# Attention decode and a gated feed-forward on one core: the last transfers are cut anew, the first query weights ride in K's row, and x's columns are made on chip

## The chip, the core and the metric

One core of one Trainium2 chip. The metric is the device time of one execution in microseconds (us). All data are float32. TensorE (PE) multiplies matrices into PSUM, VectorE (DVE) reduces and multiplies, ScalarE (ACT) does exp, square root and copies, GpSimd (POOL) sets constants, and SyncE (SP) issues nearly all transfers from HBM into SBUF.

## The reference

One token x (640 numbers) goes through an attention block over a cache of 8192 positions with 32 heads of 192, and then through a gated feed-forward of width 1536:

```
h   = x + (softmax(q K^T / sqrt(192)) V) @ wo        q = layernorm(x) @ wq, per head
h2  = h + (relu(g) * u) @ W_down                     g = layernorm(h) @ W_gate
                                                     u = layernorm(h) @ W_up
```

The caches K and V are 32 x 8192 x 192 each, so nearly all bytes are K and V, read once. The weights wq and wo are 640 x 6144 and 6144 x 640, W_gate and W_up 640 x 1536, W_down 1536 x 640.

## The kernel before

The host packs the inputs into rows, one for each of the 128 partitions. For a head there is a K row (array kk, 12288 columns, 6144 KB over all partitions) and a V row (array vv, 14208 columns, 7104 KB): V as 12 blocks of 1024 columns, then 960 columns of output weights, then 960 columns of query weights for the *next* head. The last head's V row (v0) has no query weights. A small array w0 holds the first head's query weights and x as 5 columns, and ww holds the feed-forward's weights in the order up, gate, down.

In SBUF one long tile, big, holds a K row (kt) and two V rows (vts[0], vts[1]) in turn. Head n works like this:

- TensorE makes the query from the weights at the end of the V row before (query, 5 matmuls), VectorE picks its columns out (columns), ScalarE masks them into qs (masks).
- When the K row has landed, TensorE computes the scores: 24 matmuls, each of which is two instructions in the profile, into the PSUM tile sp. The semaphore sp counts it.
- TensorE then does the output of the head *before* (output): a small matmul into po, VectorE's combine, and 8 matmuls with the output weights into acc, which counts the semaphore wo.
- VectorE takes the maximum, ScalarE the exp, and VectorE multiplies p with the 12 V blocks, one instruction each (ttr, the costly line of VectorE). The query columns of the next head come between blocks 5 and 6.

The order of the transfers is written out in sync_fn. SP issues K row n+1 when sp has counted n (the K tile is free) and V row n+1 when wo has counted n. All these transfers go into one queue and are moved in that order. Before the loop stand w0, the first K row and the first V row; after it comes the end:

- the last K row in two halves (semaphores k and k2), for which the scores wait half by half;
- the last V row in two pieces: its first JV = 7 blocks, then the other 5 with the output weights (semaphores vb and vb1);
- ww in six pieces at CUTS, issued when the scores and the output of the head before are done, since they overwrite kt and vts[0].

At the end, after the last block, the block's closing barrier passes, the last output goes into acc, ScalarE copies it to h4, the layer norm's mean and TensorE's products follow: project for up (20 matmuls into one half of sp), project for gate (20 more into the other half), VectorE's gu and its transpose guT, and 48 matmuls for down. weights() makes TensorE wait for the piece of ww that a column range begins. idle() issues matmuls whose result nobody uses. ScalarE copies the result to o4, and SP and ScalarE store it.

At the start VectorE builds constants, waits for w0 (semaphore vb) and computes the layer norm of x from the 5 columns xT with TensorE's help; x also comes as 4 rows of 160 (xrow, by ScalarE's queue) to start the sum in acc.

Of the kernel before, what the change touches and what calls it, by code (L numbers as in the profile page):

```python
# [57 lines left out]

def mha_decode_reglu_kernel(nc, x, w0, kk, vv, v0, ww, out):
    names = ("xr", "k", "k2", "va", "vb", "vb1", "qd", "qs", "sp", "mp", "pt", "m1", "rs",  # L60
             "pl", "q", "op", "po", "o", "o2", "wo", "cst", "st", "ffn0", "ffn1", "ffn2", "ffn3", "ffn4",
             "ffn5", "h4", "hm", "hc", "hr", "pu", "us", "pg", "gu", "pd", "pool", "dve")
    stored, s_o4 = (nc.alloc_semaphore("e_" + n) for n in ("out", "o4"))
# [4 lines left out]
    def sb(name, shape):  # L68
        return nc.alloc_sbuf_tensor(name, shape, F32).ap()
# [20 lines left out]
    st = sb("st", [P, 16])  # L90
# [31 lines left out]

    xT = vt2[:, 2 * VW:2 * VW + DJ]

    def ttr(eng, dst, a, b, scale, res):
# [3 lines left out]
    def sync_fn(sy):  # L129
        def load_k(h, n, dst=kt, c=slice(0, KW), sem="k"):  # L130
            if n is not None:
                sy.wait_ge(s["sp"], n)
            sy.dma_start(dst[:, c], kk[h][:, c]).then_inc(s[sem], 16)  # L133
# [6 lines left out]
        sy.dma_start(vt2[:, VW + KW + WO:2 * VW + DJ], w0).then_inc(s["vb"], 16)  # L140
        load_k(0, None)
        load_v(0, None, 0)
        sy.sem_inc(s["k2"], 16 * (H - 1))
        sy.sem_inc(s["vb1"], 16 * (H // 2))
        with sy.Fori(1, H - 2, 2) as i:
            load_k(i, i)
            load_v(i, i, 1)
            load_k(i + 1, i + 1)
            load_v(i + 1, i + 1, 0)
        load_k(H - 1, H - 1, c=slice(0, KW // 2))  # L150
        load_k(H - 1, None, c=slice(KW // 2, KW), sem="k2")
        sy.wait_ge(s["wo"], H - 1)
        for c0, c1, n in ((0, JV * SG, "vb"), (JV * SG, KW + WO, "vb1")):
            sy.dma_start(vts[1][:, c0:c1], v0[:, c0:c1]).then_inc(s[n], 16)
        sy.wait_ge(s["wo"], H)
        sy.wait_ge(s["sp"], H)
        for i, (c0, c1) in enumerate(zip(CUTS, CUTS[1:])):
            sy.dma_start(big[:, c0:c1], ww[:, c0:c1]).then_inc(s[f"ffn{i}"], 16)  # L158

# [60 lines left out]
    def vector_fn(v):  # L220
# [122 lines left out]
    def mm(dst, lhsT, rhs, start, stop, **kw):  # L343
        return nc.tensor.matmul(dst, lhsT, rhs, start=start, stop=stop, **kw)  # L344

    def weights(c0, n):
        if c0 in CUTS:
            nc.tensor.wait_ge(s[f"ffn{CUTS.index(c0)}"], 16)
        return big[:, c0:c0 + n]

    def project(c0, w0, done):
        for j in range(DJ):
            if w0 + j * F == CUTS[2]:
                idle(QB // 2)
            for g in range(NQ):
                ins = mm(sp[g * Q:(g + 1) * Q, c0:c0 + FG], hc[:, j, :], weights(w0 + j * F + g * FG, FG),
                         j == 0, j == DJ - 1)
# [19 lines left out]
    def tensor_fn(t):  # L377
# [6 lines left out]
        def scores():  # L384
            for u in range(NU):
                if u:
                    yield
# [6 lines left out]
            yield  # L394
# [17 lines left out]
        def k_wait(i, b, name):  # L412
            t.wait_ge(s[name], i * 16 + 16 * b if b else i * 16)
# [15 lines left out]
    def idle(n):  # L429
        mm(pt[:, 0:n], ident, p[:, 0:n], True, True)  # L430

    def tensor_end(t):
# [31 lines left out]

def _pack(x, k, v, wq, wo, up, gate, down):

# [3 lines left out]
    vv = _np.empty((H - 1, P, VW), v.dtype)  # L470
    v0 = _np.empty((P, KW + WO), v.dtype)
    w0 = _np.empty((P, WQ + DJ), v.dtype)
    w = wq.reshape(P, DJ, H, DH)
    o = wo.reshape(H, DH, D)
    w0[:, 0:WQ] = w[:, :, 0, :].reshape(P, WQ)
    w0[:, WQ:] = x.reshape(P, DJ)
    for h in range(H):
# [8 lines left out]
        if h < H - 1:  # L486
            r[:, KW + WO:] = w[:, :, h + 1, :].reshape(P, WQ)
    ww = _np.concatenate([a.reshape(P, -1) for a in (up, gate, down)], axis=1)
    return w0, kk, vv, v0, ww

# [22 lines left out]
```

## Time and profile before

| | |
|---|---|
| median of 3 runs | 1038.33 us (1038.3 to 1038.48) |
| the profiled execution, its own time | 1038.14 us |
| its span, first to last instruction | 1036.9 us |
| busy | PE 438.0 us (42%), DVE 525.2 us (51%), ACT 74.5 us (7%), POOL 2.8 us |
| moved | 445.98 MB, mean 430 GB/s |
| chain that ended last | DMA 76%, PE 23% |

The profile's times count from the span's start. A "busy" share is an average over the whole span. "us to landing" of a transfer counts from its issue by SP until its last bytes have landed, and so includes the time that it stands in the queue behind others. PEclk is the clock that TensorE was granted, as a part of full speed. A matrix instruction with float32 data appears twice in the profile, so 24 matmuls are 48 instructions.

### The profile page before, as it was taken

The numbers are of one execution on the slowest core, as the hardware profiler recorded it, in microseconds if no ns is written. First come the engines' busy times: TensorE is split into PE (matmuls) and PEld (weight loads), VectorE is DVE, ScalarE is ACT, GpSimd is POOL, SyncE is SP. The second block draws the span as 40 slices with busy tenths as digits, with TensorE's granted clock in tenths as the row PEclk, the third lists the DMA queues.
The fourth block names the chain that finished last, engine by engine and source line by source line (L and its number), as shares of the span: only waits on it lengthen the run. The fifth ranks groups of instructions, "written<-read, shape, count | busy, mean of one in ns | idle before, by whom it ended". The sixth has DMA issues, their size and how long they took to land.

```text
span 1036.9 us, 7438 instructions
## 1 busy us (share of the span) xinstructions
PE 438.0 (42%) x2746; PEld 201.2 (19%) x2746; DVE 525.2 (51%) x1162; ACT 74.5 (7%) x174; POOL 2.8 (0%) x18
## 2 busy tenths in 40 slices
PE   4255343344443344443443443443433553433536
PEld 2122121122121121111221111221211221211203
DVE  1644465644555544556544556444656444656472
ACT  1000000000000000000000000000000000000001
POOL 1000000000000000000000000000000000000000
PEclk8566666666655666655666655666656666656667
DMA  9999999999999999999999999999999999999998
GB/s 402 450 423 432 432 427 449 420 428 432 434 449 420 449 430 432 432 420 451 419 432 432 431 449 420 427 434 436 446 420 451 423 432 432 424 451 420 427 435 346
DMA packets 10532, 445.98 MB, mean 430 GB/s; under 512 B 1176, under 2 KB 1184, under 8 KB 1568
## 3 DMA queue, kind: packets, MB, share of 16 engines
q1 hardware_dynamic: 10516, 445.92, 99.6%
q8 instruction: 3, 0.05, 0.0%
q14 instruction: 1, 0.01, 0.0%
q10 hardware_dynamic: 12, 0.00, 0.0%
HBM read 445.91 MB, written 0.00 MB: 430 GB/s over the span
## 4 chain that ended last, share of the span: by engine, by line
DMA 76%; PE 23%; issue 0%; SPq 0%; DVE 0%; ACT 0%
DMA big<-in_kk_dram 72%; PE sp L344 23%; DMA big<-in_ww_dram 3%; SPq L133 0%; SPq L158 0%; PE pq L344 0%; PE acc L344 0%; SPq L140 0%; DVE junk L126 0%; PE po L344 0%; ACT o L340 0%; DVE o L126 0%
## 5 line engine op out<-in xcount | busy, mean ns | idle before, releaser
L126 DVE CUSTOM_DVE_ANT_0 big<-big,p 128x1024 f32<-128x1024 f32 x384 | 444.9, 1220 | 146.5 <-DMA big<-in_vv_dram 145.3
L344 PE MATMUL sp<-big,qs 128*32 128x512 f32 x1536 | 239.9, 789 | 342.9 <-DMA big<-in_kk_dram 338.4
L344 PE MATMUL pq<-big,xn 128*128 128x192 f32 x320 | 113.4, 540 | 154.2 <-DMA big<-in_vv_dram 152.3
L344 PEld LDWEIGHTS sp<-big,qs 128*32 128x32 f32 x1536 | 55.9, 140 | 513.4 <-DMA big<-in_kk_dram 359.7
L126 DVE CUSTOM_DVE_ANT_0 junk<-blk,po,rl 128x8 f32<-128x8 f32 x66 | 11.9, 218 | 265.5 <-PE po L344 265.5
L344 PEld LDWEIGHTS pq<-big,xn 128*128 128x128 f32 x320 | 97.9, 331 | 157.0 <-DMA big<-in_vv_dram 155.0
L303 ACT ACTIVATE o<-side,o 128x64 f32<-128x64 f32 x33 | 11.5, 348 | 479.2 <-DVE o L126 479.2
L315 ACT ACTIVATE qs<-pick,q 128x64 f32<-128x64 f32 x33 | 11.5, 348 | 410.3 <-DVE q L126 410.3
L321 ACT ACTIVATE p<-sp,m 128x1024 f32<-128x1024 f32 x32 | 35.6, 1113 | 47.9 <-DVE m L259 47.9
L257 DVE TENSOR_REDUCE mp<-sp 128x1 f32<-128x1024 f32 x32 | 39.0, 1220 | 0.0
L344 PE MATMUL pl<-rs,share 128*128 128x1 f32 x64 | 16.5, 327 | 51.9 <-ACT p L321 51.9
L261 DVE RECIPROCAL rl<-pl 128x1 f32<-128x1 f32 x32 | 5.4, 169 | 59.0 <-PE pl L344 59.0
L344 PE MATMUL acc<-big,o 128*32 128x160 f32 x528 | 28.8, 316 | 15.3 <-DVE o L126 15.3
L126 DVE DVE_READ_ACCUMULATOR2_ANT op<- 128x1 f32 x384 | 31.4, 82 | 0.0
L344 PEld LDWEIGHTS pl<-rs,share 128*128 128x128 f32 x64 | 13.8, 268 | 58.0 <-ACT p L321 58.0
L344 PE MATMUL po<-op,same 128*128 128x12 f32 x66 | 13.1, 272 | 16.0 <-PEq L452 16.0
L344 PEld LDWEIGHTS po<-op,same 128*128 128x128 f32 x66 | 10.0, 191 | 42.9 <-issue 26.8
L259 DVE TENSOR_REDUCE m<-pt 128x1 f32<-128x128 f32 x32 | 9.3, 292 | 13.3 <-PE pt L408 13.3
L344 PEld LDWEIGHTS acc<-big,o 128*32 128x32 f32 x528 | 10.6, 108 | 25.8 <-DVE o L126 18.4
L408 PE MATMUL pt<-ident,mp 128*128 128x128 f32 x32 | 10.3, 323 | 8.9 <-DVE mp L257 8.9
L126 DVE CUSTOM_DVE_ANT_0 junk<-ident,pq 128x128 f32<-128x128 f32 x33 | 9.3, 282 | 3.7 <-PE pq L344 3.7
L316 ACT ACTIVATE qs<-pick,q 128x32 f32<-128x32 f32 x33 | 10.1, 307 | 0.0
(78 smaller groups left out, 73.8 us busy)
## 6 DMA issues: line engine op xcount, KB each, us to landing
big<-in_vv_dram SPq DMA_DIRECT2D x31, 7104.0 KB, 38.8
big<-in_kk_dram SPq DMA_DIRECT2D x31, 6144.0 KB, 23.6
big<-in_kk_dram SPq DMA_DIRECT2D x2, 3072.0 KB, 19.5
big<-in_ww_dram SPq DMA_DIRECT2D x1, 3840.0 KB, 20.3
big<-in_v_dram SPq DMA_DIRECT2D x1, 3584.0 KB, 30.2
big<-in_v_dram SPq DMA_DIRECT2D x1, 3040.0 KB, 37.1
big<-in_ww_dram SPq DMA_DIRECT2D x1, 2304.0 KB, 25.5
big<-in_ww_dram SPq DMA_DIRECT2D x1, 2176.0 KB, 30.2
```

Source lines behind the costliest of these rows:

```text
L126: return eng.tensor_tensor_reduce(out=res, in0=a, in1=b, scale=scale, scalar=0.0, op0=ALU.mult, op1=ALU.add, accum_out=dst)
L257: v.reduce_max(mp, sp, axis=AX.X).then_inc(s["mp"])
L259: v.reduce_max(m1, pt[:, 0:P], axis=AX.X, negate=True).then_inc(s["m1"])
L261: v.reciprocal(rl, pl[:, 0:1])
L303: a.mul(o2, side, o[:, 1:2]).then_inc(s["o2"])
L315: a.mul(qs[:, 0:2, :], pk[:, 0:2, :], q[:, 0:1])
L316: a.mul(qs[:, 2, :], pk[:, 2, :], q[:, 1:2]).then_inc(s["qs"])
L321: a.activation(p, sp, AF.Exp, bias=m1, accum_out=rs).then_inc(s["rs"])
L344: return nc.tensor.matmul(dst, lhsT, rhs, start=start, stop=stop, **kw)
L408: t.transpose(pt[:, 0:P], mp.to_broadcast([P, P]), ident).then_inc(s["pt"])
```

## The change

*The long tile is laid out anew*: vts[1], then kt, then vts[0]. The query weights at the end of vts[1] and kt are now neighbours, and so are vts[1]'s output weights and the space behind them.

*The start.* w0 is gone. The first K row comes with the first head's query weights ahead of it, as one transfer k0 (13248 columns, 6624 KB) on the semaphore vb. x's columns are made on chip: VectorE multiplies the mask quad with xrow into a new tile xd, and five one-column matmuls with ones put x's columns into po, from which the layer norm reads.

*The end.* The last K row is one transfer. The last V row is cut at JV = 10 blocks, and its second piece now carries the up weights behind the output weights (10688 columns). That piece reaches into kt, so SP waits for the last scores (sp at H) before it, and no longer before ww. ww holds gate and down alone, in four pieces. project takes the up weights without a wait, and the filler ahead of gate's fourth row of matmuls is gone.

SP's queue at the start and at the end, before (names are tile <- input array, then partitions x columns; the first V row and the loop's transfers lie between the two pieces):

```order
L140 DMA big<-in_w_dram 128x965
L133 DMA big<-in_kk_dram 128x12288
...
L133 DMA big<-in_kk_dram 128x6144 [waits e_sp]
L133 DMA big<-in_kk_dram 128x6144
L154 DMA big<-in_v_dram 128x7168 [waits e_wo]
L154 DMA big<-in_v_dram 128x6080
L158 DMA big<-in_ww_dram 128x7680 [waits e_sp,e_wo]
L158 DMA big<-in_ww_dram 128x4608
L158 DMA big<-in_ww_dram 128x4352
L158 DMA big<-in_ww_dram 128x3840
L158 DMA big<-in_ww_dram 128x1920
L158 DMA big<-in_ww_dram 128x640
```

and of the change:

```order
L141 DMA big<-in_k_dram 128x13248
...
L134 DMA big<-in_kk_dram 128x12288 [waits e_sp]
L152 DMA big<-in_v_dram 128x10240 [waits e_wo]
L154 DMA big<-in_v_dram 128x10688 [waits e_sp]
L157 DMA big<-in_ww_dram 128x8960 [waits e_wo]
L157 DMA big<-in_ww_dram 128x3840
L157 DMA big<-in_ww_dram 128x1920
L157 DMA big<-in_ww_dram 128x640
```

The wait for the scores has moved from ww to the second V piece, and 7680 columns of up weights have moved ahead of ww's first wait.

TensorE's order at the feed-forward, before, from the last output's mean to the first down matmuls:

```order
L344 MATMUL pt<-hs,ones 128x1 [waits e_h4]
L344 MATMUL sp<-big,hc 32x384 [waits e_ffn0,e_hc]
L344 MATMUL sp<-big,hc 32x384 x3
L344 MATMUL pl<-st,ones 128x1 [waits e_st]
L344 MATMUL sp<-big,hc 32x384 x16
L344 MATMUL sp<-big,hc 32x384 [waits e_ffn1]
L344 MATMUL sp<-big,hc 32x384 x11
L344 MATMUL pt<-p,ident 128x256
L344 MATMUL sp<-big,hc 32x384 [waits e_ffn2]
L344 MATMUL sp<-big,hc 32x384 x7
```

and of the change:

```order
L347 MATMUL pt<-hs,ones 128x1 [waits e_h4]
L347 MATMUL sp<-big,hc 32x384 [waits e_hc]
L347 MATMUL sp<-big,hc 32x384 x3
L347 MATMUL pl<-st,ones 128x1 [waits e_st]
L347 MATMUL sp<-big,hc 32x384 x16
L347 MATMUL sp<-big,hc 32x384 [waits e_ffn0]
L347 MATMUL sp<-big,hc 32x384 x19
```

Up no longer waits for a piece of ww, gate waits for one piece instead of two, and the filler within gate is gone.

The diff, cut to its core:

```diff
-JV = 7
-GATE, DOWN, FW = DJ * F, 2 * DJ * F, 2 * DJ * F + FJ * D
-CUTS = (0, GATE, GATE + 3 * F, DOWN + 2 * D, DOWN + 8 * D, DOWN + 11 * D, FW)
+JV = 10
+UP = DJ * F
+VL = KW + WO + UP
+GATE, DOWN, FW = 0, DJ * F, DJ * F + FJ * D
+CUTS = (0, DOWN + 2 * D, DOWN + 8 * D, DOWN + 11 * D, FW)
...
-    big = sb("big", [P, KW + 2 * VW + DJ])
-    kt, vt2 = big[:, 0:KW], big[:, KW:]
-    vts = [vt2[:, i * VW:(i + 1) * VW] for i in range(2)]
+    big = sb("big", [P, VW + KW + VW])
+    kt = big[:, VW:VW + KW]
+    vts = [big[:, VW + KW:], big[:, 0:VW]]
+    upw, ffn = big[:, KW + WO:VL], big[:, VL:VL + FW]
     xrow = sb("xrow", [NQ, DG])
+    xd = sb("xd", [NQ, DJ, NQ, Q])
...
-        sy.dma_start(vt2[:, VW + KW + WO:2 * VW + DJ], w0).then_inc(s["vb"], 16)
-        load_k(0, None)
+        sy.dma_start(big[:, KW + WO:VW + KW], k0).then_inc(s["vb"], 16)
         load_v(0, None, 0)
...
-        load_k(H - 1, H - 1, c=slice(0, KW // 2))
-        load_k(H - 1, None, c=slice(KW // 2, KW), sem="k2")
+        load_k(H - 1, H - 1)
         sy.wait_ge(s["wo"], H - 1)
-        for c0, c1, n in ((0, JV * SG, "vb"), (JV * SG, KW + WO, "vb1")):
-            sy.dma_start(vts[1][:, c0:c1], v0[:, c0:c1]).then_inc(s[n], 16)
+        sy.dma_start(big[:, 0:JV * SG], v0[:, 0:JV * SG]).then_inc(s["vb"], 16)
+        sy.wait_ge(s["sp"], H)
+        sy.dma_start(big[:, JV * SG:VL], v0[:, JV * SG:VL]).then_inc(s["vb1"], 16)
         sy.wait_ge(s["wo"], H)
-        sy.wait_ge(s["sp"], H)
         for i, (c0, c1) in enumerate(zip(CUTS, CUTS[1:])):
-            sy.dma_start(big[:, c0:c1], ww[:, c0:c1]).then_inc(s[f"ffn{i}"], 16)
+            sy.dma_start(ffn[:, c0:c1], ww[:, c0:c1]).then_inc(s[f"ffn{i}"], 16)
...
+        v.wait_ge(s["xr"], 16)
+        v.tensor_mul(xd, quad.rearrange("q (o g i) -> q o g i", o=1, g=NQ).to_broadcast([NQ, DJ, NQ, Q]),
+                     xrow.rearrange("q (i o j) -> q j o i", o=1, j=DJ).to_broadcast([NQ, DJ, NQ, Q])).then_inc(s["xd"])
...
-        v.wait_ge(s["vb"], 16)
+        xT = po[:, 0:DJ]
+        v.wait_ge(s["xd"], 2)
...
-    def project(c0, w0, done):
+    def project(c0, w, done):
         for j in range(DJ):
-            if w0 + j * F == CUTS[2]:
-                idle(QB // 2)
...
-            sc = scores()
-            k_wait(i, b, "k")
-            next(sc)
-            k_wait(i, b, "k2")
-            next(sc)
+            t.wait_ge(s["k"], i * 16 + 16 * b if b else i * 16)
+            scores()
...
+        t.wait_ge(s["xd"], 1)
+        for j in range(DJ):
+            ins = mm(po[:, j:j + 1], xd[:, j].rearrange("q g i -> q (g i)"), ones[0:NQ, 0:1], True, True)
+        ins.then_inc(s["xd"])
...
-        project(0, 0, "pu")
-        project(QB, GATE, "pg")
+        project(0, lambda n: upw[:, n:n + FG], "pu")
+        project(QB, lambda n: weights(GATE + n, FG), "pg")
```

More of the change, by code (lines that the diff above doesn't have):

```diff
@@ L56, in sync, with mha_decode_reglu_kernel @@
         self.eng.wait_ge(self.c.sem, self.c.n)
[L59 to L62, printed above, removed]
+def mha_decode_reglu_kernel(nc, x, k0, kk, vv, v0, ww, out):
+    names = ("xr", "xd", "k", "va", "vb", "vb1", "qd", "qs", "sp", "mp", "pt", "m1", "rs",
+             "pl", "q", "op", "po", "o", "o2", "wo", "cst", "st", "ffn0", "ffn1", "ffn2", "ffn3",
+             "h4", "hm", "hc", "hr", "pu", "us", "pg", "gu", "pd", "pool", "dve")
     stored, s_o4 = (nc.alloc_semaphore("e_" + n) for n in ("out", "o4"))
@@ L129, in sync_fn, with load_k @@
     def sync_fn(sy):
[L130 to L133, printed above, removed]
+        def load_k(h, n):
+            sy.wait_ge(s["sp"], n)
+            sy.dma_start(kt, kk[h - 1]).then_inc(s["k"], 16)
         def load_v(h, n, b):
@@ L138, in load_v @@
             sy.dma_start(vts[b], vv[h]).then_inc(s["vb" if b else "va"], 16)
-        sy.dma_start(vt2[:, VW + KW + WO:2 * VW + DJ], w0).then_inc(s["vb"], 16)
-        load_k(0, None)
+        sy.dma_start(big[:, KW + WO:VW + KW], k0).then_inc(s["vb"], 16)
         load_v(0, None, 0)
-        sy.sem_inc(s["k2"], 16 * (H - 1))
+        sy.sem_inc(s["k"], 16)
         sy.sem_inc(s["vb1"], 16 * (H // 2))
@@ L348, in weights @@
             nc.tensor.wait_ge(s[f"ffn{CUTS.index(c0)}"], 16)
-        return big[:, c0:c0 + n]
-    def project(c0, w0, done):
+        return ffn[:, c0:c0 + n]
+    def project(c0, w, done):
         for j in range(DJ):
-            if w0 + j * F == CUTS[2]:
-                idle(QB // 2)
             for g in range(NQ):
-                ins = mm(sp[g * Q:(g + 1) * Q, c0:c0 + FG], hc[:, j, :], weights(w0 + j * F + g * FG, FG),
-                         j == 0, j == DJ - 1)
+                n = j * F + g * FG
+                ins = mm(sp[g * Q:(g + 1) * Q, c0:c0 + FG], hc[:, j, :], w(n), j == 0, j == DJ - 1)
             if j == 0 and c0 == 0:
@@ L462, in mha_decode_reglu_kernel, with _pack @@
     sync_end(nc.sync)
-def _pack(x, k, v, wq, wo, up, gate, down):
+def _pack(k, v, wq, wo, up, gate, down):
     import numpy as _np
@@ L470, in _pack @@
     vv = _np.empty((H - 1, P, VW), v.dtype)
-    v0 = _np.empty((P, KW + WO), v.dtype)
-    w0 = _np.empty((P, WQ + DJ), v.dtype)
+    v0 = _np.empty((P, VL), v.dtype)
+    k0 = _np.empty((P, WQ + KW), k.dtype)
     w = wq.reshape(P, DJ, H, DH)
     o = wo.reshape(H, DH, D)
-    w0[:, 0:WQ] = w[:, :, 0, :].reshape(P, WQ)
-    w0[:, WQ:] = x.reshape(P, DJ)
     for h in range(H):
@@ L487, in _pack @@
             r[:, KW + WO:] = w[:, :, h + 1, :].reshape(P, WQ)
-    ww = _np.concatenate([a.reshape(P, -1) for a in (up, gate, down)], axis=1)
-    return w0, kk, vv, v0, ww
+    k0[:, 0:WQ] = w[:, :, 0, :].reshape(P, WQ)
+    k0[:, WQ:] = kk[0]
+    v0[:, KW + WO:] = up.reshape(P, UP)
+    ww = _np.concatenate([a.reshape(P, -1) for a in (gate, down)], axis=1)
+    return k0, kk[1:], vv, v0, ww
 def kernel(**inputs):
@@ L499 @@
          ("A_x", "A_k_cache", "A_v_cache", "A_wq", "A_wo", "B_W_gate", "B_W_up", "B_W_down")}
-    w0, kk, vv, v0, ww = _pack(a["A_x"], a["A_k_cache"], a["A_v_cache"], a["A_wq"], a["A_wo"], a["B_W_up"],
+    k0, kk, vv, v0, ww = _pack(a["A_k_cache"], a["A_v_cache"], a["A_wq"], a["A_wo"], a["B_W_up"],
                                a["B_W_gate"], a["B_W_down"])
-    ins = {"x": a["A_x"], "w0": w0, "kk": kk, "vv": vv, "v0": v0, "ww": ww}
+    ins = {"x": a["A_x"], "k0": k0, "kk": kk, "vv": vv, "v0": v0, "ww": ww}
     nc = _bacc.Bacc("TRN2", target_bir_lowering=False, num_devices=1)
```

6 lines of the change are left out of this document (removed).

## The prediction

> **What bounds the kernel now.** I read the page's slices first, then the chain of work that ended last, then the DMA issues, then the timeline of the last 70 us. The slices show the transfers busy from end to end, with a fall only in the last slice:
>
> ```profile
> DMA  9999999999999999999999999999999999999998
> GB/s 402 450 423 432 432 427 449 420 428 432 434 449 420 449 430 432 432 420 451 419 432 432 431 449 420 427 434 436 446 420 451 423 432 432 424 451 420 427 435 346
> ```
>
> So the bytes set the time, and a change can only act on what stands before the stream, behind it, or in a gap that it opens. The chain (start, length, what) shows how a head works and how the end works:
>
> ```profile
> 0.81 0.42 SPq L140
> ...
> 1.28 17.59 DMA big<-in_kk_dram
> ...
> 208.13 6.72 PE sp L344 x48
> ...
> 396.07 8.32 PE sp L344 x48
> ...
> 959.92 8.00 PE sp L344 x48
> ...
> 968.32 22.95 DMA big<-in_kk_dram
> 991.32 2.78 PE sp L344 x24
> ...
> 997.60 36.20 DMA big<-in_ww_dram
> 1033.85 1.34 PE pq L344 x32
> 1035.21 0.30 ACT o L340
> ```
>
> The last K row lands at 968.32 + 22.95 = 991.27. The last but one piece of ww lands at 1033.80, and the remaining 3.1 us are the last 32 matmul instructions, ScalarE's copy and the store. The same 48 score instructions take 6.72 us in one head and 8.32 us in another, which matters below. The DMA issues give KB and time from issue to landing:
>
> ```profile
> big<-in_v_dram SPq DMA_DIRECT2D x1, 3584.0 KB, 30.2
> big<-in_v_dram SPq DMA_DIRECT2D x1, 3040.0 KB, 37.1
> big<-in_ww_dram SPq DMA_DIRECT2D x1, 3840.0 KB, 20.3
> big<-in_ww_dram SPq DMA_DIRECT2D x1, 960.0 KB, 36.2
> big<-in_w_dram SPq DMA_DIRECT2D x1, 482.5 KB, 3.5
> big<-in_ww_dram SPq DMA_DIRECT2D x1, 320.0 KB, 36.5
> ```
>
> And the timeline shows the compute chain that runs beside the last transfers (start, length, engine, line, operation):
>
> ```profile
> 969.57 0.80 SPq L154 DMA_DIRECT2D big<-in_v_dram  x2
> 995.80 2.70 SPq L158 DMA_DIRECT2D big<-in_ww_dram  x6
> 998.38 0.17 DVE L261 RECIPROCAL rl<-pl 128x1 f32<-128x1 f32 x1 [1.71 <-PE pl L344]
> 999.81 1.22 DVE L126 CUSTOM_DVE_ANT_0 big<-big,p 128x1024 f32<-128x1024 f32 x1 [1.26 <-DMA big<-in_v_dram]
> 1011.62 1.22 DVE L126 CUSTOM_DVE_ANT_0 big<-big,p 128x1024 f32<-128x1024 f32 x1
> 1013.92 0.08 DVE L126 DVE_READ_ACCUMULATOR2_ANT op<- 128x1 f32 x1
> 1017.53 0.59 PE L344 MATMUL pt<-hs,ones 128*128 128x1 f32 x2 [0.87 <-ACT h L333]
> 1018.71 1.51 PE L344 MATMUL sp<-big,hc 128*32 128x384 f32 x8 [0.59 <-DVE hc L287]
> 1020.66 5.96 PE L344 MATMUL sp<-big,hc 128*32 128x384 f32 x56
> 1027.17 1.50 PE L344 MATMUL sp<-big,hc 128*32 128x384 f32 x16
> 1028.82 0.56 DVE L298 SCALAR_TENSOR_TENSOR gu<-sp,us 128x384 f32<-128x384 f32 x1 [6.46 <-PE sp L344]
> 1030.49 0.75 PE L344 MATMUL pq<-big,guT 128*32 128x160 f32 x16
> 1031.54 1.84 PE L344 MATMUL pq<-big,guT 128*32 128x160 f32 x48 [0.29 <-DMA big<-in_ww_dram]
> 1033.85 1.29 PE L344 MATMUL pq<-big,guT 128*32 128x160 f32 x32 [0.47 <-DMA big<-in_ww_dram]
> ```
>
> The reader is to see two clocks here. V's first piece is issued at 969.57 and lands 30.2 us later, at 999.77; VectorE starts its 12 blocks at 999.81 and ends at 1014.00 (1013.92 + 0.08), whatever lands meanwhile. From there the chain up, gate, gu, down runs with little to spare: it waits for ww at 1031.54 and 1033.85, and behind filler matmuls at 1027.17. Without those waits it would end only about 2 us earlier (worked out below): the slack that the stream leaves it.
>
> **The change, part by part.**
>
> *Fewer transfers.* Ten transfers of the end become seven, and w0 goes into K's row: four fewer for the same bytes (w0's 2.5 KB of x apart). What does one transfer cost in a full queue? The 320 KB piece is issued 0.45 us behind the 960 KB piece (2.70 us for six issues), so it lands 0.45 + 36.5 - 36.2 = 0.75 us behind it. At the rate of V's first piece, 3584 KB in 999.77 - 991.27 = 8.50 us or 421.6 KB/us, its bytes alone take 0.76. So a transfer costs about nothing, at most 0.15 us with the rounding of these rows. At the start, w0 lands at 0.81 + 3.5 = 4.3 and K lands at 18.87, 14.57 us later: 6144 KB at 421.7 KB/us, no gap either. I put all four at 0.3 us before the last V row (bounds 0 and 0.6): K lands at 990.97.
>
> The Trainium skill speaks otherwise. "DMA: Bandwidth & Descriptors", section "Anatomy of one DMA", puts a fixed cost of some 2 us on each DMA (fitted on the GpSimd path), and its rules tell authors to coalesce many small transfers. Four of them would be an estimated 8 us by that page; this trace disagrees with it for a queue that is never empty, with 0.75 us for the whole of a 320 KB piece. The sum does without it; the rival below takes its price from a row.
>
> *The first head.* The query now waits for the whole first row:
>
> ```profile
> 9.61 3.47 PE L344 MATMUL pq<-big,xn 128*128 128x192 f32 x10 [1.93 <-DVE xn L246]
> 13.85 0.31 ACT L316 ACTIVATE qs<-pick,q 128x32 f32<-128x32 f32 x1
> 35.67 1.22 DVE L126 CUSTOM_DVE_ANT_0 big<-big,p 128x1024 f32<-128x1024 f32 x1 [4.69 <-DMA big<-in_vv_dram]
> ```
>
> Query, columns and masks took 14.16 - 9.61 = 4.55 us and lay under K's transfer; now they follow it. Scores end at the latest at 18.9 + 4.6 + 8.3 = 31.8, and only then does SP, whose next instruction is that wait, issue the second K row; V's next row is behind it in the same queue. The first V row lands at 35.67, so 3.9 us of cover are left (9 us before). A transfer's lead from an empty queue is at most the 3.5 us of w0, of which its bytes are 1.1. So this costs nothing; without cover it would cost each us that is missing. Making x's columns (one VectorE product, five one-column matmuls) lies under 18 us of transfer: nothing.
>
> *The last head.* K as one row: 48 score instructions follow its landing instead of 24. By the bounds 6.72 and 8.32 they end between 997.7 and 999.3 (994.10 before). SP then issues V's second row, for which the new wait stands; behind it in SP's queue wait the four ww transfers. V's first row, now 5120 KB, keeps the stream busy until 990.97 + 12.14 = 1003.1, so at least 3.8 us are left for the issue: no gap. VectorE's reciprocal ended 4.45 us after the scores (994.10 to 998.55), now by 1003.7 at the latest, so the first ten blocks may start 0.6 us after their data: ten blocks and the columns between them took 1011.62 - 999.81 = 11.81 us, so until 1015.5.
>
> *The last V row.* It carries two V blocks, the output weights and the 3840 KB up weights. 5120 + 5344 = 10464 KB at 421.6 KB/us are 24.82 us: it lands at 1015.79. VectorE, done with ten blocks by 1015.5, waits for it, then needs 0.04 and two blocks, 1014.00 - 1011.62 = 2.38: done at **1018.21, 4.21 us later than now**. This is the term that decides. The up weights, of which the chain had no need until 1018.7, now stand ahead of V's last two blocks, which it needs first.
>
> *From there.* The chain's links keep their lengths where they didn't wait for ww. From the last block to the first up matmul: 1018.71 - 1014.00 = 4.71, so 1022.92. Up and gate: 64 instructions ended at 1026.62, 7.91 us after that; the other 16 are four groups of four at 0.32 (at full clock 20 weight loads stand in 1.60 us, in the stretches below): 9.2, and gu begins 0.15 later, at 1032.27. No wait: gate lands with the first ww piece, 4480 KB or 10.6 us behind V, at 1026.4. gu to the first down matmul: 1030.49 - 1028.82 = 1.67, so 1033.94. Down: 96 instructions; 48 took 1.84 and 32 took 1.29, so 16 more cost 0.55, and 96 are 1.84 + 3 x 0.55 = 3.49. All pieces but the last have landed by then, and the last, at about 1034.1, before its turn. ScalarE's copy starts 0.07 later, at 1037.50, and from its start to the end of the span it was 1036.90 - 1035.21 = 1.69. Sum: 1039.19, **if TensorE's clock rises as late as it did**.
>
> *The clock.* The granted clock in that stretch:
>
> ```profile
> 1018.70:1020.20 1.50, 1.50 (x9) 0.26 (x9) 0.31 (x2) 0.00 (x0) 0.00 (x0) 0.50 1.04 441
> 1020.20:1023.20 3.00, 3.00 (x20) 1.23 (x22) 1.17 (x7) 0.29 (x1) 0.00 (x0) 0.50 0.99 424
> 1023.20:1024.80 1.60, 1.60 (x24) 0.60 (x20) 0.00 (x0) 0.00 (x0) 0.00 (x0) 1.00 1.00 416
> ```
>
> It was 0.50 (the number before DMA's share) for 4.5 us of matmuls and 1.00 then. Each us at half clock costs half a us. The scores' 6.72 to 8.32 us for equal work show how far this wanders: 24 of them at full clock take 2.78, so 48 about 5.3, and the rest, 1.4 to 3.0 us, stands for 3 to 6 us at half clock. The end wanders likewise, by 0.8 us either way. I take 3.6 us at half clock instead of 4.5, because the scores come after an idle TensorE and here 0.59 us of matmuls (1017.53) go ahead and may count: 0.45 off, **1038.74**.
>
> The Trainium skill, "TensorE: Matmul & The Clock Gate", section "What's actually happening", says that the activity window is 3413 ns long and free-running, not started with the kernel. The trace agrees with the width (about 3 us between the shortest and the longest), and by that rule one run's phase says nothing about the next.
>
> Against the span of 1036.9 that is +1.84, so 1038.14 + 1.84 = 1039.98 for the profiled execution; the median of the runs shown, 1038.33, stands 0.19 above it, so about **1040.1** with half of that.
>
> **The rivals.**
>
> 1. *The clock rises late (slower).* Place: the up matmuls. Half a us for each us beyond 3.6; at 6 us it gives 1041.3. It decides from 4.2 us on: there the time passes 1040.41, 0.2% over the median. For it: the 4.5 us of this very execution. Against it: the matmuls ahead, and that a median over runs takes the middle phase.
> 2. *A gap in the queue (slower).* The second V row waits for all 48 scores. It needs over 3.8 us from issue to first bytes; then each us more is a us later, say 1041.5. Against it: w0's 3.5 us to its landing.
> 3. *The stream sets the end as before (faster).* If the chain behind V were over 2 us shorter than its rows say, the last piece would decide, 0.4 us earlier: 1037.7. Against it: each link has its row, and nothing in the change shortens one.
> 4. *Each transfer saved is a lead saved (faster).* That is what it would be if w0's 3.5 us less its 1.1 of bytes were paid by each: 4 x 2.4 = 9.6, or 1028.7. Against it: the 0.75 us piece. The skill's fixed cost would come out near this.
>
> **How the numbers follow.** My forecast, the late V row with the clock rising within 4.2 us, has 0.54 and 1039.2 to 1040.4 as its own range; rival 1 has 0.33, rival 2 0.04, rival 3 0.07, rival 4 0.02. 0.2%, about what a measurement of this kernel can tell from no change, is 2.08 us, and the forecast lies inside it, though on the slow side. Faster 0.09, within 0.54, slower 0.37. The range: 0.8 for an early clock and 0.3 for the upper bound of the transfers below, as much above, each rounded outward by 0.1: 1038.9 to 1041.3; rivals 3 and 4 and most of 2 stay outside.
>
> **What would show it.** Right: VectorE idle for V's second row before its last two blocks, the last of them ending near 1018.2; no wait for ww from up to down; the chain that ended last going through VectorE's last blocks instead of ww. Wrong: a DMA share below 9 tenths near 1003 or near 35 us, waits for ww among the down matmuls, or VectorE reaching block ten after its data.

## The result, and the profile after

The changed kernel takes **1041.61 us** (median of 8 runs, 1040.39 to 1042.18), the kernel before 1038.43 (8 runs beside them, 1038.3 to 1038.56): ratio 1.003, 95% interval [1.002, 1.0039]. It is slower by 3.18 us, or 0.3%. I had predicted 1040.1 and a range up to 1041.3. The profiled execution took 1041.6, its span is 1040.2 (before 1038.14 and 1036.9), so the span grew by 3.3.

The slices of the page after: the queue is full as before, with a fall in the last slice that is deeper than it was (309 GB/s, before 346).

```profile
DMA  9999999999999999999999999999999999999997
GB/s 401 420 443 433 437 421 447 421 429 438 437 436 430 439 427 431 430 443 426 443 428 437 432 428 441 419 435 438 439 426 441 428 431 431 430 447 419 443 418 309
```

The chain that ended last, as far back as the profile follows it, which is to the end of VectorE's last block (start, length, what). No DMA stands in this stretch, where before a piece of ww did; what came ahead of it is read from the timeline below.

```profile
1019.51 0.59 PE po L347 x2
1020.53 0.35 ACT o L306
1020.89 1.28 ACT L334
1022.39 0.28 ACT h L336 x2
1023.89 1.50 PE sp L347 x8
1025.40 0.52 PE pl L347 x2
1025.92 7.27 PE sp L347 x72
1033.18 1.49 PE pt L347 x4
1034.67 3.85 PE pq L347 x104
1038.54 0.30 ACT o L343
```

And the timeline of the changed kernel, first and last head:

```profile
19.61 3.57 PE L347 MATMUL pq<-big,xn 128*128 128x192 f32 x10 [8.37 <-DMA big<-in_k_dram]
31.99 0.34 SPq L134 DMA_DIRECT2D big<-in_kk_dram  x1
...
992.05 8.22 PE L347 MATMUL sp<-big,qs 128*32 128x512 f32 x48 [11.05 <-DMA big<-in_kk_dram]
1000.34 0.33 SPq L154 DMA_DIRECT2D big<-in_v_dram  x1
1004.69 1.23 DVE L128 CUSTOM_DVE_ANT_0 big<-big,p 128x1024 f32<-128x1024 f32 x1
...
1016.50 0.08 DVE L128 DVE_READ_ACCUMULATOR2_ANT op<- 128x1 f32 x1
1016.80 1.22 DVE L128 CUSTOM_DVE_ANT_0 big<-big,p 128x1024 f32<-128x1024 f32 x1 [0.22 <-DMA big<-in_v_dram]
1019.10 0.08 DVE L128 DVE_READ_ACCUMULATOR2_ANT op<- 128x1 f32 x1
1023.89 1.50 PE L347 MATMUL sp<-big,hc 128*32 128x384 f32 x8 [0.59 <-DVE hc L290]
...
1033.34 0.56 DVE L301 SCALAR_TENSOR_TENSOR gu<-sp,us 128x384 f32<-128x384 f32 x1 [5.80 <-PE sp L347]
1035.01 3.47 PE L347 MATMUL pq<-big,guT 128*32 128x160 f32 x96
1038.54 0.30 ACT L343 ACTIVATE o<-pq 128x160 f32<-128x160 f32 x1 [7.86 <-PE pq L347]
```

Three readings. The last K row is first used at 992.05; before, its second half was at 991.32. VectorE's last block, behind a wait of 0.22 us for the V row's second piece, ends at 1019.10 + 0.08 = 1019.18; before it was 1014.00. And from up to the end nothing waits for ww: the 80 matmul instructions and the 96 of down run through. The difference of the spans adds up from these rows: up starts 1023.89 - 1018.71 = 5.18 later, from there gu comes after 9.45 instead of 10.11, the copy after gu by 5.20 instead of 6.39, the end after the copy as before: 5.18 - 0.66 - 1.19 = 3.33. The chain had some 2 us of slack (the 0.66 and 1.19 that its waits cost before) and was made 5.2 us later.

The clock while up and gate run (from:to, length, busy time and count of PE, PEld, DVE, ACT, POOL, then the granted clock, DMA share, GB/s):

```profile
1023.90:1028.50 4.60, 4.60 (x30) 1.58 (x34) 1.46 (x9) 0.29 (x1) 0.00 (x0) 0.50 1.00 428
1028.50:1033.10 4.60, 4.60 (x60) 1.54 (x52) 0.00 (x0) 0.58 (x1) 0.00 (x0) 0.99 0.95 394
```

### The profile page after: what moved, and what is told of

Its sections match the earlier page's. It is cut to its first block, busy times and chain, and to the rows that moved or that the text cites. A ratio compares the mean times of both kernels' runs of the same rounds, so it can differ in the third digit from the quotient of the medians.

```text
span 1040.2 us, 7450 instructions
## 1 busy us (share of the span) xinstructions
PE 437.8 (42%) x2754; PEld 203.8 (20%) x2754; DVE 526.5 (51%) x1163; ACT 74.5 (7%) x174; POOL 2.8 (0%) x18
```

## The experiments

All times are medians; each ratio is against the kernel before, run beside it on the same chip. Of each edit the core is shown. Where it helps, a table at the end of this section gives the landmarks of the last head.

**The start alone** (e1): the kernel before, with the change's start and long tile, and the old end.

```diff
-        sy.dma_start(vt2[:, VW + KW + WO:2 * VW + DJ], w0).then_inc(s["vb"], 16)
-        load_k(0, None)
+        sy.dma_start(big[:, KW + WO:VW + KW], k0).then_inc(s["vb"], 16)
         load_v(0, None, 0)
```

> The change's start on the end of the kernel before: one first row of 53 KB a partition, x's columns made on chip, the query behind that row; K in halves, V cut at 7 blocks, ww in six pieces as before. Theory A (the start itself loses time: the first row landed at 19.57 in the changed kernel, w0 and K at 18.87 before, and every later landing is 0.7 late): first row lands near 19.6, all later K rows 0.7 later than before, time 1038.4 + 0.7 = 1039.1. Rival B (the start is made good in the queue, and the 3.2 us come from the end alone): 1038.4.

1038.73 (10 runs), 1.0006 [0.9996, 1.0015]. The first row is used at 19.78, against 18.91 for K in the trace of before (e1, then before):

```profile
19.78 3.57 PE L347 MATMUL pq<-big,xn 128*128 128x192 f32 x10 [8.54 <-DMA big<-in_k_dram]
```

```profile
18.91 7.41 PE L344 MATMUL sp<-big,qs 128*32 128x512 f32 x48 [5.83 <-DMA big<-in_kk_dram]
```

The time moves by less than can be told; the landing moves by 0.9. The start is no gain, and most of the 3.2 us is elsewhere.

**The end alone** (e2): the change, with the first row cut in two transfers again, query weights first.

```diff
-        sy.dma_start(big[:, KW + WO:VW + KW], k0).then_inc(s["vb"], 16)
+        sy.dma_start(big[:, KW + WO:VW], k0[:, 0:WQ]).then_inc(s["vb"], 16)
+        sy.dma_start(kt, k0[:, WQ:]).then_inc(s["k"], 16)
```

> The change's end with the start cut in two again (the query weights as a first transfer of 480 KB, then K; x's columns still made on chip). Theory A: K lands near 18.9, everything 0.7 earlier than in the changed kernel, 1041.6 - 0.7 = 1040.9, with a spread of over a us from run to run, since the compute chain sets the end and TensorE's clock rises at another time in each run. Rival B: 1041.6.

1041.38 (8 runs), 1.0029 [1.0018, 1.004]. The end costs nearly all of it. But the cut did not restore the start: K is first used at 19.45, not at the 18.9 that I expected. The query weights are still read out of the long rows of k0, which the later runs show to matter.

**A small first transfer** (e3): e1, with 64 columns sent ahead, in case the long first packets held the queue back.

```diff
-        sy.dma_start(big[:, KW + WO:VW + KW], k0).then_inc(s["vb"], 16)
+        sy.dma_start(big[:, KW + WO:KW + WO + 64], k0[:, 0:64]).then_inc(s["k"], 16)
+        sy.dma_start(big[:, KW + WO + 64:VW + KW], k0[:, 64:]).then_inc(s["vb"], 16)
```

> As e1_start_only, but a first transfer of 64 columns (256 bytes a partition) goes ahead of the rest of the first row. The query still waits for the whole row. If the loss comes of each DMA engine's first packet being 53 KB long (theory A1: they took 2 to 3.6 us in the changed kernel, 1.96 later), the small packets take that up and the row lands by 18.9: 1038.4. If it comes of the query that waits for the row, or of the longer row itself (rival A2), the small piece changes nothing: row at 19.6, 1039.1.

1039.09 (10 runs), 1.0008 [0.9998, 1.0018], and the row is used at 20.06. So small packets at the front do not cure it; they too are read out of the long rows.

```profile
20.06 3.57 PE L347 MATMUL pq<-big,xn 128*128 128x192 f32 x10 [8.81 <-DMA big<-in_k_dram]
```

**The up weights behind V** (e4): the change, but V's second piece ends with the output weights, and up follows as a transfer of its own.

```diff
-        sy.dma_start(big[:, JV * SG:VL], v0[:, JV * SG:VL]).then_inc(s["vb1"], 16)
+        sy.dma_start(big[:, JV * SG:KW + WO], v0[:, JV * SG:KW + WO]).then_inc(s["vb1"], 16)
+        sy.dma_start(upw, v0[:, KW + WO:VL]).then_inc(s["up"], 16)
```

> The changed kernel with the second V row's piece cut in two: the two V blocks and output weights first, the up weights behind them as a transfer and a semaphore of their own. Theory C (the prediction's term: the up weights ahead of V's last blocks push the chain back): V lands 9 us earlier, VectorE ends about 4 us earlier, the stream sets the end again: about 1039.2. Rival D (two bounds nearly together: VectorE can't begin the last head's blocks before 1004.7, since K is one row and the scores end at 1000.2, and twelve blocks take 14.2): last block at 1018.9 instead of 1019.2, 1041.3.

1041.04 (10 runs), 1.0026 [1.0016, 1.0036]. If the up weights alone set the end, VectorE's last block would have ended some 4 us earlier and the time been about 1039.2; the block ended 0.64 us earlier, at 1018.54. The timeline of e4 says why: VectorE no longer waits for V's second piece, but it begins the first ten blocks at 1004.36, straight behind the reciprocal of the late scores.

```profile
1004.22 0.17 DVE L265 RECIPROCAL rl<-pl 128x1 f32<-128x1 f32 x1 [1.71 <-PE pl L348]
1004.36 1.23 DVE L128 CUSTOM_DVE_ANT_0 big<-big,p 128x1024 f32<-128x1024 f32 x1
...
1018.46 0.08 DVE L128 DVE_READ_ACCUMULATOR2_ANT op<- 128x1 f32 x1
```

**And K's row in halves again** (e6): e4, with the last K row cut as before, so that half the scores lie under the other half's transfer.

```diff
-        load_k(H - 1, H - 1)
+        load_k(H - 1, H - 1, slice(0, KW // 2))
+        load_k(H - 1, None, slice(KW // 2, KW), "k2")
```

> As e4_up_behind, and the last K row in two halves again, so that the scores end 5 us earlier, near 994.7. Three bounds theory (D, sharpened): VectorE's first block of the last head then waits no longer for the scores but for the V row's first piece of 5120 KB, which lands 12.1 us behind K, near 1003.9; so it begins 0.5 us earlier than in e4 and the end moves by that alone: 1040.6. Rival (the scores behind one K row were the whole delay): VectorE begins 4 us earlier, the stream sets the end, 1039.

1040.86 (10 runs), 1.0022 [1.0012, 1.0031]. The scores end at 995.18, five us earlier than in the change, and VectorE still starts at 1004.51: now it waits for V's first piece, ten blocks in one transfer. I had expected it 0.5 us earlier than in e4. Counted from the first use of the last K row it is that, 12.11 us against 12.60; but K came 0.64 later in this profile (992.40, in e4 991.76).

```profile
992.40 2.78 PE L351 MATMUL sp<-big,qs 128*32 128x512 f32 x24 [1.24 <-DMA big<-in_kk_dram]
1004.51 1.23 DVE L128 CUSTOM_DVE_ANT_0 big<-big,p 128x1024 f32<-128x1024 f32 x1 [4.88 <-DMA big<-in_v_dram]
...
1018.62 0.08 DVE L128 DVE_READ_ACCUMULATOR2_ANT op<- 128x1 f32 x1
```

**And V cut at seven blocks** (e12): e6 with JV = 7, and the wait for the scores behind the second V piece.

```diff
-JV = 10
+JV = 7
...
-        sy.wait_ge(s["sp"], H)
         sy.dma_start(big[:, JV * SG:KW + WO], v0[:, JV * SG:KW + WO]).then_inc(s["vb1"], 16)
+        sy.wait_ge(s["sp"], H)
```

> As e6_up_behind_khalf, and the last V row cut at 7 blocks again, with the up weights still behind V as a transfer of their own and the changed kernel's start. Three bounds theory (D): only now, with the third bound gone, does VectorE begin earlier: first piece of V near 1000.4, last block near 1014.6, 4 us earlier than in e6; the stream sets the end, and the time is that of e1, 1038.8. Rival (the end is slow for another reason, such as fewer and longer pieces of ww): it stays near e6, 1040.8.

1039.33 (10 runs, 1038.86 to 1041.88), 1.0014 [1.0005, 1.0024]. Now VectorE is four us earlier than in e6, and within 0.8 us of the kernel before. Undone one on top of the other, the three bounds gave way only with the last. The time is still 0.5 us above the 1038.8 that I expected, and two of the ten runs took 1041.14 and 1041.88. What is left of the loss is in part the start, which e12 keeps, and in part a new wait: gate comes in one piece of ww, and TensorE stands still for it (timeline of e12).

```profile
1000.53 1.23 DVE L128 CUSTOM_DVE_ANT_0 big<-big,p 128x1024 f32<-128x1024 f32 x1 [1.04 <-DMA big<-in_v_dram]
...
1014.64 0.08 DVE L128 DVE_READ_ACCUMULATOR2_ANT op<- 128x1 f32 x1
1027.62 3.43 PE L351 MATMUL sp<-big,hc 128*32 128x384 f32 x40 [1.60 <-DMA big<-in_ww_dram]
```

**V cut at seven blocks alone** (e7): the change with the one number, so that the second piece, issued behind the scores as in the change, has less V ahead of it.

```diff
-JV = 10
+JV = 7
```

> The changed kernel with the last V row cut at 7 blocks instead of 10, all else the same: five blocks now lie in the piece with the up weights. Theory (the piece with the up weights lands near 1016.8 wherever the cut is, and each block in it stands behind that landing at 1.15 us): last block at 1016.8 + 5.8 = 1022.6 instead of 1019.2, time 1041.6 + 3.4 = 1045.0. Rival (the end is set by VectorE's total work from 1004.7 on, and the cut doesn't matter): 1041.6.

1047.68 (2 runs), 1.0089 [1.0071, 1.0108]: worse than I expected. The second piece is issued at 999.95, and VectorE waits for it until 1019.12 (timeline, then windows of e7):

```profile
999.95 0.33 SPq L154 DMA_DIRECT2D big<-in_v_dram  x1
...
1012.85 0.08 DVE L128 DVE_READ_ACCUMULATOR2_ANT op<- 128x1 f32 x1
1019.12 1.22 DVE L128 CUSTOM_DVE_ANT_0 big<-big,p 128x1024 f32<-128x1024 f32 x1 [6.19 <-DMA big<-in_v_dram]
```

```profile
998.00:1000.00 2.00, 2.00 (x22) 0.54 (x14) 0.00 (x0) 0.00 (x0) 0.00 (x0) 1.00 0.10 43
1000.00:1002.00 2.00, 1.26 (x19) 0.55 (x18) 1.51 (x5) 0.35 (x1) 0.00 (x0) 1.00 1.44 440
```

A DMA share of 0.10 for two us: the queue is nearly dry until the issue. Shares of stretches this short are coarse, as the 1.44 shows; over 990 to 1016 the share is 0.89 in e7 and 0.97 in the change. The second piece is used 1019.12 - 1016.80 = 2.3 us later than in the change. The other 3.4 us are the three more blocks that stand behind it, at 1.15 each: the last one ends at 1024.94, 5.76 later than in the change, and the span is 5.9 longer. This is the gap of the prediction's second rival. In the change itself V's ten blocks cover it, as the prediction said; at seven they don't.

**Matmuls to raise the clock** (e8): the change, with 13 filler matmuls of 512 columns while VectorE works, and three more in the links between (of 128, 512 and 128 columns), so that TensorE isn't idle ahead of up. The fillers compute nothing that is used.

```diff
-    def idle(n):
-        mm(pt[:, 0:n], ident, p[:, 0:n], True, True)
+    def idle(n, dst=None):
+        mm((pt if dst is None else dst)[:, 0:n], ident, p[:, 0:n], True, True)
...
+        for _ in range(13):
+            idle(QB)
...
-        output(t, H + 1, vts[1])
+        output(t, H + 1, vts[1], lambda n: idle(n, pq))
```

> The changed kernel with 13 filler matmuls of 512 columns on the idle TensorE while VectorE works on the last head's blocks, and three short ones in the gaps of the chain behind them, so that the clock is up when the up matmuls begin. Theory (half of the time at half clock, 4.7 us here, is lost in the chain, and the moment at which the clock rises makes the spread from run to run): no matmul of up at half clock, down reached 2.5 us earlier, the stream sets the end again: 1038.9, with a spread of a few tenths. Rival (the clock matters little, the chain's lengths are VectorE's and ScalarE's): 1041.3 with the same spread of nearly 2 us.

1039.61 (10 runs, 1038.94 to 1040.18), 1.0011 [1.0002, 1.0021]. The time fell by 2.0 us, not by the 2.7 expected, and the runs still spread over 1.2 us, not over a few tenths. The profile of e8 shows up and gate at full clock throughout, and shows why less came back than expected: the clock fell to 0.50 between, and the filler behind the output projection took 2.08 us and pushed up to 1024.12 (timeline, then windows of e8).

```profile
1021.24 2.08 PE L347 MATMUL pq<-p,ident 128*128 128x512 f32 x2
1024.12 0.85 PE L347 MATMUL sp<-big,hc 128*32 128x384 f32 x8 [0.22 <-DVE hc L290]
...
1033.05 3.47 PE L347 MATMUL pq<-big,guT 128*32 128x160 f32 x96
```

```profile
1024.10:1031.20 7.10, 7.08 (x83) 2.74 (x83) 1.49 (x9) 0.88 (x2) 0.00 (x0) 1.00 0.94 394
1020.10:1023.40 3.30, 3.30 (x21) 1.59 (x21) 0.47 (x1) 2.01 (x5) 0.00 (x0) 0.50 1.03 445
```

That gives the price of the clock: from the first matmul of up to the first of down it took 8.93 here (1024.12 to 1033.05) against 11.12 in the change (1023.89 to 1035.01), 2.2 us, about half of the 4.7 that the change spent at 0.50.

**What costs 0.7 us at the start?** Seven more runs, all but the last two with the old end. The first (e5) is e1 with the first row cut as in e2, so that the query again goes ahead of K:

```diff
-        sy.dma_start(big[:, KW + WO:VW + KW], k0).then_inc(s["vb"], 16)
+        sy.dma_start(big[:, KW + WO:VW], k0[:, 0:WQ]).then_inc(s["vb"], 16)
+        sy.dma_start(kt, k0[:, WQ:]).then_inc(s["k"], 16)
```

> As e1_start_only, but the first row is cut in two again: the query weights as a transfer of their own ahead of K, so that the query no longer waits for K; x's columns still made on chip. If the start's loss comes of the merged first transfer and the late query behind it (theory A), this is the kernel before but for x's columns: 1038.4. If it comes of something else in the start, such as the columns made on chip or which DMA engine happens to begin late (rival A3), it stays near e1: 1038.7 to 1039.1.

1038.77 (11 runs), 1.0004 [0.9995, 1.0013]; K is used at 19.39. So the loss needs neither the merging nor the late query. Whether the merging adds to it stays open: with the first row in one piece the row is used at 19.50 to 20.06 in nine profiles, with it cut K is used at 19.39 and 19.45 (e5, e2). The next (e9) is the kernel before with only x's columns made on chip, w0 holding the query weights alone:

```diff
-    w0 = _np.empty((P, WQ + DJ), v.dtype)
+    w0 = _np.empty((P, WQ), v.dtype)
```

> The kernel before with one part of the change alone: x's columns made on chip, w0 without them (960 columns, a contiguous array of its own), all transfers, their order and the tile's layout as before. Theory A4 (the 0.4 us that e1 and e5 lost come of how the first bytes lie in HBM, query weights in K's long rows, and not of the columns): 1038.35, no different from before. Rival (the columns made on chip cost them): 1038.75.

1038.28 (11 runs), 1.0 [0.9991, 1.0009]; K is used at 18.90. Making the columns is free, as predicted. Then (e10) the kernel before once more, unchanged, for the scatter of that landing.

> The kernel before, profiled on the chip of e9, as a measure of how much the landing of the first rows varies between chips: if the start of the kernel before is the same everywhere, K lands near 18.9 and the second K row near 51.4 as in the first profile; if chips differ, the second K row lands near 51.8 to 52.1 as in e1 to e8, and the changed kernel's late start in its own profile is in part the chip's.

1038.44 in one run; K is used at 19.16, so two profiles of the same kernel on two chips differ by 0.25 there. Then (e11) e5 with the query weights in an array of their own, so that only the change's layout of the long tile and x's columns are left:

```diff
-    k0 = _np.empty((P, WQ + KW), k.dtype)
+    w0 = _np.empty((P, WQ), v.dtype)
...
-        sy.dma_start(big[:, KW + WO:VW], k0[:, 0:WQ]).then_inc(s["vb"], 16)
-        sy.dma_start(kt, k0[:, WQ:]).then_inc(s["k"], 16)
+        sy.dma_start(big[:, KW + WO:VW], w0).then_inc(s["vb"], 16)
+        sy.dma_start(kt, kk[0]).then_inc(s["k"], 16)
```

> As e5_split_start (new layout of the long tile, x's columns on chip, query weights and K as two transfers), but the query weights come from a contiguous array of their own and the first K row from the array of all K rows, as in the kernel before. If where the first bytes lie in HBM costs the 0.4 us of e1 and e5 (theory A4): 1038.35. If the tile's new layout costs them: 1038.75, as in e5.

1038.22 (11 runs), 1.0 [0.9991, 1.0009]; K is used at 18.89. The layout is free. And (e15) e11 with K alone read out of the long rows:

```diff
-        sy.dma_start(kt, kk[0]).then_inc(s["k"], 16)
+        sy.dma_start(kt, k0[:, WQ:]).then_inc(s["k"], 16)
```

> As e11_layout_only (query weights from a contiguous array of their own), but the first K row still from the array in which each partition's row is 52992 bytes long and begins with the query weights, which are skipped. If K's rows at that stride cost the 0.4 us of e1 and e5: 1038.7. If it is the query weights read in 3840-byte pieces 53 KB apart, or at the head of one long row: 1038.3.

1038.17 (11 runs), 0.9998 [0.9989, 1.0007]; K is used at 19.11. The stride of K is free too. What is left between e5 and e15 is one thing: whether the 3840 bytes of query weights of a partition are read from an array of their own or from the heads of rows 53 KB long. The packets in the kept traces put the delay there too: the 128 packets of query weights take 30.8 us in total in e5 (32.2 in e2) and the last of them ends at 4.49 (4.55 in e2); in the six profiles with an array of their own they take 25.6 to 27.9 and end between 3.95 and 4.20. K's 128 packets behind them take the same in both, 232.7 to 234.3. The first use of K in each timeline (e5, e9, e10, e11, e15 in this order):

```profile
19.39 7.84 PE L347 MATMUL sp<-big,qs 128*32 128x512 f32 x44 [2.63 <-DMA big<-in_k_dram]
```

```profile
18.90 7.05 PE L347 MATMUL sp<-big,qs 128*32 128x512 f32 x48 [2.33 <-DMA big<-in_kk_dram]
```

```profile
19.16 7.94 PE L344 MATMUL sp<-big,qs 128*32 128x512 f32 x48 [5.98 <-DMA big<-in_kk_dram]
```

```profile
18.89 7.25 PE L347 MATMUL sp<-big,qs 128*32 128x512 f32 x48 [2.13 <-DMA big<-in_kk_dram]
```

```profile
19.11 5.36 PE L347 MATMUL sp<-big,qs 128*32 128x512 f32 x48 [2.34 <-DMA big<-in_k_dram]
```

Last, the change itself with e11's start (e13), beside the change again on the same chip (e14). The edit of e13; e14 is the changed kernel without one:

```diff
-        sy.dma_start(big[:, KW + WO:VW + KW], k0).then_inc(s["vb"], 16)
+        sy.dma_start(big[:, KW + WO:VW], w0).then_inc(s["vb"], 16)
+        sy.dma_start(kt, kk[0]).then_inc(s["k"], 16)
```

> The changed kernel with the start of e11: query weights in a contiguous array of their own, the first K row from the array of all K rows, two transfers. If the start's cost adds to the end's (theory), it is 0.4 us faster than the changed kernel on the same chip: 1041.6 - 0.4 = 1041.2, and the end alone is worth +2.8. Rival (the start's lateness is absorbed, since the compute chain sets the end): no difference, 1041.6.

> The changed kernel as it is, on the same chip as e13, as its reference: 1041.6 with a spread of nearly 2 us, the end falling with the time that TensorE stays at half clock (2.3 to 6 us). Rival for the clock (it rises early because of the matmuls ahead of up, as the prediction took it, 3.6 us): mean below 1041.2.

e13: 1040.71 (10 runs), 1.0023 [1.0014, 1.0032]. e14: 1041.59 (7 runs), 1.0031 [1.0019, 1.0042]. By the medians the end costs 2.4 us and the start 0.9 (by the means 2.4 and 0.6). The two intervals overlap, so that the sizes of the parts are not sharp; that the end is slower by itself is clear. The mean of e14, 1041.4, also speaks against the early clock (below 1041.2). The first rows land as the reason says, at 18.96 with the array of its own and at 19.50 out of the long rows (timelines of e13 and e14):

```profile
18.96 6.79 PE L347 MATMUL sp<-big,qs 128*32 128x512 f32 x48 [2.19 <-DMA big<-in_kk_dram]
991.14 7.09 PE L347 MATMUL sp<-big,qs 128*32 128x512 f32 x48 [10.97 <-DMA big<-in_kk_dram]
```

```profile
19.50 3.57 PE L347 MATMUL pq<-big,xn 128*128 128x192 f32 x10 [8.26 <-DMA big<-in_k_dram]
991.54 8.00 PE L347 MATMUL sp<-big,qs 128*32 128x512 f32 x48 [11.26 <-DMA big<-in_kk_dram]
```

The last head of the kernels that tell its bounds apart (us in each one's profile; the last column is the time of up and gate at a clock of 0.50, read from windows like those above):

| kernel | scores end | VectorE's first block | its last block ends | up starts | span | at 0.50 |
|---|---|---|---|---|---|---|
| before | 994.10 | 999.81 | 1014.00 | 1018.71 | 1036.9 | 4.5 |
| the change | 1000.27 | 1004.69 | 1019.18 | 1023.89 | 1040.2 | 4.7 |
| e4, up behind V | 999.93 | 1004.36 | 1018.54 | 1023.25 | 1039.7 | 4.9 |
| e6, and K in halves | 995.18 | 1004.51 | 1018.69 | 1023.41 | 1040.0 | 5.2 |
| e12, and V cut at 7 | 994.84 | 1000.53 | 1014.71 | 1019.42 | 1038.1 | 5.8 |
| e13, weights in an array of their own | 998.24 | 1003.24 | 1018.27 | 1022.99 | 1039.9 | 5.9 |

## Why the prediction missed

The mechanism was as predicted in the main: the late V row made the compute chain set the end. The time was 1.5 us above the forecast. Step by step:

- *The queue is full, and fewer transfers save little.* Right, and even the little was wrong. "I put all four at 0.3 us before the last V row (bounds 0 and 0.6): K lands at 990.97." K was first used at 992.05, some 0.05 behind its landing: **the step that failed first**, by about 1.0 us, and its sign with it. I bounded the gain from below at nothing, and so left no room for a cost, although k0's first bytes were read in a way that no row of before showed. The 0.3 of gain is not shown either: in the six profiles with the weights in an array of their own, the last K row is used between 991.14 (e13, the only one with the new end) and 991.47 (991.32 in the kernel before). In the runs the cost goes with the query weights at the heads of the long rows: K is first used between 18.89 and 19.16 in these six profiles (before, e9, e10, e11, e13, e15), and the first row or K between 19.39 and 20.06 in the other eleven. In time, e1 and e5 alone are inconclusive; the two groups of landings, which don't overlap, and e13 beside e14 carry this. Why such reads are slower stays open.
- *The first head costs nothing.* Right where I looked: x's columns are free (e9), and the late scores still let SP issue in time (31.99). Its weights' transfer was the hidden cost.
- *VectorE done at 1018.21, 4.21 us later.* The link held: 1019.18, and its excess of 0.97 is the late K row's. But the sentence "this is the term that decides. The up weights [...] now stand ahead of V's last two blocks" names one of three bounds that lie within 0.64 us: VectorE waited for that row just 0.22 us in the change. Whole-row scores and ten blocks in the first piece hold its end at almost the same place (1018.54 in e4, 1018.69 in e6), and only with all three undone is it 4.5 us earlier (e12). My sum had the ten blocks ready at 1015.5 and the row at 1015.79, so it did show the near tie; I read it as one cause.
- *From there.* But for up and gate, which the clock lengthened, each link within 0.05: to up 4.71, gu to down 1.67, down to the copy 3.53 (I had 3.56), copy to the end about 1.7. No wait for ww, as foretold.
- *The clock.* "I take 3.6 us at half clock instead of 4.5": the change had 4.69, 0.54 us of time. **The second step that failed.** Over the sixteen profiles without e8's fillers, this time was 3.8 to 6.0, 4.9 on average; e13, whose matmuls ahead of up are those of the change, had 5.85. My 0.45 off was a credit for the short matmuls ahead of up (1017.53). But that row is one of before: the same matmuls, 2.46 us of the 4.71 ahead of up there and 2.45 here, were already ahead of its 4.5, which came out in spite of them. The prediction's own reading of the scores, 3 to 6 us, had 4.5 in its middle too. The windows of e13, over that stretch and then up and gate at 0.50:

```profile
1018.27:1022.99 4.72, 2.46 (x21) 1.55 (x21) 1.32 (x9) 2.11 (x5) 0.00 (x0) 0.50 0.85 364
...
1022.99:1028.84 5.85, 5.85 (x38) 1.94 (x42) 1.47 (x9) 0.29 (x1) 0.00 (x0) 0.50 1.01 426
```

The Trainium skill, "TensorE: Matmul & The Clock Gate", section "What's actually happening", lets the clock rise after at least one busy window of about 3.4 us; with the free-running window that the prediction already cites, that makes an estimated 3.4 to 6.8 us from the first matmul, 5.1 in the middle. The 3.8 to 6.0 measured agree: the middle of that range would have been nearer than the one row that I moved.

- *The sum.* 0.97 + 0.54 - 0.03 bring 1038.74 to 1040.22; the span measured is 1040.2. Of the 1.5 us the late K row is about 1.0, of which 0.3 is the gain that did not come and 0.7 the start's cost, and the clock 0.5. In the medians of e14 and e13 the start is worth 0.9.

Of the rivals, the first (the clock rises late) came in part: 4.69 is past the 4.2 at which I said that it decides. At its price it gives 1040.6, so it does not reach the time measured by itself. Rival 2's gap exists, but only at the cut of e7. Rivals 3 and 4 are out: the stream did not set the end, and no transfer saved a lead.

## What to carry to other kernels

In a queue that never ran dry, as here, fewer transfers were worth nothing that could be seen; what counts is which bytes stand ahead of what the last compute chain waits for, and how much slack that chain has (here 2 us, and each of the three bounds alone spends four or five). Bounds that end within a us of each other hide one another, so undoing one shows nothing: undo them together, or read each one's landing in the timeline. When a compute chain takes the end over from a transfer, the time that its matmuls spend at half clock becomes part of the end and varies from run to run, and the middle of that time (4.9 us here), not a value below every row at hand, belongs in the sum.

## What the runs showed of the hardware that was not expected

- 480 KB of weights read from the heads of 53 KB rows, as the first transfer, made the first K row 0.7 us later on average than the same bytes from an array of their own (19.39 to 20.06 in eleven profiles against 18.89 to 19.16 in six). A 53 KB stride of K itself cost nothing (e15, 19.11).
- A queue can run nearly dry before its last piece has landed: in e7 that piece was issued at 970.55 and landed 30.0 us later, 0.6 us after the next issue at 999.95. Yet the DMA share was 0.10 over the two us ahead of that issue, and the next piece came 2.3 us later than in the change.
- The scatter: 1.8 us between the change's runs against 0.3 between those of before. The half-clock time's own 2.2 us, at half a us each, would be 1.1 of it; with up and gate at full clock in its profile, e8 still scatters by 1.2. Where the rest comes from stays open.
- A raised clock can fall behind a short gap: in e8 TensorE had no matmul from 1016.4 to 1019.19, the clock fell to 0.50 at about 1020.1, with matmuls running again, and was 1.00 again by 1024.1.
